# Attention and a squared-ReLU FFN in one planned order: batch 0's last P.V part, x turned pair by pair, and new constants of the planner

## The chip, the cores and the metric

The kernel runs on one core of a Trainium2 chip. The metric is the device time of one execution in microseconds (us), as the median of several runs. The core has a matrix engine (TensorE; PE in the profile, with its weight loads as PEld), VectorE (DVE), ScalarE (ACT), GpSimd (POOL) and SyncE (SP). Matrix products land in PSUM, of which the kernel uses eight banks of 128 x 512 fp32; DVE and ACT take them from there to SBUF. DMAs are issued here from POOL (nearly all loads, which turn fp32 into fp16 on the way), from SP (outputs, transposing DMAs, a few first loads) and from ACT (a few first loads).

## The reference, cut to what matters

Attention with a bias that depends on the distance of query and key, over 8 batches, 8 heads, 576 positions and head size 64; its heads laid side by side are the input of a two-layer FFN whose activation is the square of a ReLU.

```python
scores = scale * np.matmul(q, k.transpose(0, 1, 3, 2))      # q, k, v: 8 x 8 x 576 x 64
scores = scores + bias.transpose(2, 0, 1)[None, :, :, :]    # bias_table[bucket(|i - j|)]
attn = np.exp(scores - max); attn = attn / attn.sum(-1)
x = np.matmul(attn, v).transpose(0, 2, 1, 3).reshape(4608, 512)
h = np.maximum(x @ w_in, 0.0)                               # w_in: 512 x 2048
out = h * h @ w_out                                         # w_out: 2048 x 512
```

## The kernel before, in words

**The attention** goes by pairs of heads: pair p = 4 b + hp holds heads 2 hp and 2 hp + 1 of batch b, 32 pairs in all (`pair`, line 580). For each pair:

- q and k are loaded into a staging buffer (five of them, taken in order) and turned, so that the head size lies on the partitions. In batches 0 to 2 PE turns them with transposes (line 608): 12 of 96 x 64 for each of q and k, into a bank of the ring `r_g`, from which ACT or DVE copies them to SBUF (`copy_to`, lines 570 and 572). From batch 3 on, a transposing DMA of SP does it. POOL or DVE copies some 64 x 64 corners into `qz` (line 635). Pair 0's q and k come by their own loads as fp32 and are cast (lines 468 and 470).
- The scores are made by PE in the two banks-of-two `st` (lines 653, 677, 702) and taken through exp by ACT (lines 664, 687, 712) into `pt` and `pm`: four exps of 128 x 1024, one of 512 and one of 576 per pair.
- DVE multiplies them with exp(bias), only where keys and queries are near (four products per pair, line 745). The tables for it are built once at the start: far bias (326), 96 small matmuls (353) in six banks of `r_g`, copied to `tb_sb` by ACT or DVE (365, 367), and `tm_sb` (374).
- P.V is made by PE in two parts, query tiles 0 to 2 and 3 to 4 (lines 781 and 788), one after the other in the only bank `pv`, the row sums coming along as a 65th column. After each part DVE takes the reciprocal (805) and the product with it (810) into `x`.

**x** is then turned for the layers. In batches 0 to 2 (`x_turn`, line 838) this is done once per batch, after its fourth pair: for each of the five query tiles, four transposes, one per pair, into one bank of `r_g` (848), and one copy of up to 512 columns to `xt`. From batch 3 on SP's transposing DMA does it.

**The layers** go by nine groups of 512 tokens (`layers`, line 1026). Layer 1 of a group is 16 tiles; a tile is four matmuls over `kk`, that is over the four pairs of a batch, into one bank of `r_g` (1044), then ReLU by ACT or, in the first two groups, DVE (1065, 1067), then the square by DVE (1075). Layer 2 (`second`, line 929) uses a scheme with seven instead of eight products of 2 x 2 blocks, each product 16 matmuls (962). Sums of the activations (921) and of the weights (901) are made by DVE beforehand. Products 1 and 2, 5 and 3, and 7 and 4 follow one another in one bank each; 2, 3 and 4 have to wait until the one before has been read (989, 995, 997). Their order is `P_ORDER`, and `P_LAST` for the last group. Layer 2 of group g - 1 is interleaved with layer 1 of group g.

The ring `r_g` has three banks, and serves q and k turns, tables, x turns, layer 1 and layer 2 alike.

**The order of everything** is made before the program is built. Each piece of work is an `Op` with a cost per engine, what it depends on, the buffers that it takes, a due time and possibly an `after`, before which it may not be planned. `Plan.schedule` (line 106) advances each engine by itself and takes the op that can start first, and among several the one with the least due time. Ops that name two engines go to the one that can start first. The result is one fixed order on each engine. A pair's due time is `nominal(p)` = LEAD + FAST min(p, FASTN) + PERIOD max(p - FASTN, 0), its `after` is AHEAD earlier; group g is due at G0 + GP g. These constants set the priorities, and the costs in the `P.add` calls set the planner's clock; neither is a wait on the chip. The fills (memsets of constant regions, line 388, by DVE) have due times and `after` values of their own (QUIET, LATER, and 25000 for those of the staging buffers, line 405). The loads of POOL follow a list: those of batch 0, then `ORDER`, in which k0 and k1 are k of pairs 4, 5 and of pairs 6, 7 (q0 and q1 likewise), i0 to i3 quarters of w_in, o0 to o3 of w_out, and v the six loads of v of batch 1.

Of the kernel before, what the change touches and what calls it, by code (L numbers as in the profile page):

```python
# [25 lines left out]
GT = 512  # L26
# [4 lines left out]
PERIOD, LEAD, FAST, FASTN = 9600.0, 1600.0, 3000, 7  # L31
AHEAD, G0, GP = 20600.0, 54700.0, 35900.0
# [3 lines left out]
QUIET, LATER = 5200.0, 8500.0  # L36
TAB, EV = 6400.0, 1
P_ORDER = "1 6 2 5 7 3 4"
P_LAST = "1 6 2 5 7 3 4"
SIX = 3  # L40
ORDER = "k0 i0 q0 q1 v i1 i2 o0 k1 o1 i3 o2 o3"
# [149 lines left out]
def kernel(  # L191
# [74 lines left out]
    def loader(eng_name, eng, out_, in_, packets, deps=(), bufs=(), due=0.0):  # L266

        lane = [Buf(r_lane)] if eng_name == "POOL" else []
        issue = P.add(
            {eng_name: 720.0 if eng_name == "POOL" else 600.0},  # L270
            lambda: io(eng.dma_start(out=out_(), in_=in_())),  # L271
            deps,
            list(bufs) + lane,
            due,
        )
        return P.add({"DMA": packets / 16}, None, [issue], list(bufs) + lane, due if lane else -1e9), issue
# [9 lines left out]
    def load(eng_name, eng, out_, in_, packets, deps=(), bufs=(), due=0.0):  # L286
        return loader(eng_name, eng, out_, in_, packets, deps, bufs, due)[0]
# [15 lines left out]
        128 * 27, due=0,  # L303
# [21 lines left out]
        {"PE": 250.0},  # L325
# [21 lines left out]
    for c in range(6):  # L347
# [11 lines left out]
        o = P.add({"PE": 16 * 55.0}, t_mm, [o_eb, l_oh], [t_b], LEAD + TAB, 0.0, "f")  # L359
# [27 lines left out]
    def fill(ap, value, ns, due, after, deps=()):  # L387
# [3 lines left out]
    z_fix = [[fill(zz[:, 0], 0.0, 150.0, 10, QUIET)], [fill(zz[:, 1:], 0.0, 300.0, 11, LATER)]]  # L391
    first = [
        fill(pt_sb[:, :, PW:], 1.0, 150.0, 20, LATER),
        fill(pm_sb[:, :, S:], 1.0, 150.0, 20, LATER),
# [11 lines left out]
        fill(stg[i][w][96:128, 512:640].bitcast(FP32), 0.0, 90.0, 40 + i, 25000.0)  # L406
# [56 lines left out]
    def cast_first(w):  # L463

        def cast(o):
            src, dst = first_f[0:96, ts(w, 768)], stg[b_stg[0].slot][w][0:96, :]
# [95 lines left out]
    xt_ready, x_last = {}, {}  # L562
# [17 lines left out]
    def pair(p):  # L580
# [5 lines left out]
        for w, dst in ((0, qts), (1, kts)):  # L586
# [14 lines left out]
            def tr(w=w, bank=bank):  # L601
                ps = g_ps[bank.slot].bitcast(FP16)
                t = stg[b_stg[p].slot][w]
                if b < SIX:
# [11 lines left out]

            o = P.add({"PE": 12 * 36.0 if b < SIX else 5 * mm(128)}, tr, l_qk[p, w] + [l_id], [bank, b_stg[p]], T - 3000, after, "c" if b < SIX else "f")

# [152 lines left out]
        for part, qt0, nq in ((0, 0, 3), (1, 3, 2)):  # L771
            bank = Buf(r_pv)

            def pv(qt0=qt0, nq=nq, bank=bank):
                ps = pv_ps[bank.slot][:, 0 : nq * 130].rearrange("p (t e d) -> p t e d", t=nq, e=2)
# [27 lines left out]
            def recip(nq=nq, bank=bank, rb=rb):  # L803
                ps = pv_ps[bank.slot][:, 0 : nq * 130].rearrange("p (t e d) -> p t e d", t=nq, e=2)
                io(nc.vector.reciprocal(out=rs[rb.slot][:, 0:nq], in_=ps[:, :, :, 64:65]))

            def norm(nq=nq, bank=bank, rb=rb, qt0=qt0):
                ps = pv_ps[bank.slot][:, 0 : nq * 130].rearrange("p (t e d) -> p t e d", t=nq, e=2)
# [29 lines left out]
    def x_turn(b, norms):  # L838
        xb = [x_bufs[4 * b + hp] for hp in range(4)]
        T = nominal(4 * b + 3)  # L840
        for qt in range(5):
            n = 128 if qt < 4 else 64
            bank = Buf(r_g)

            def tr(qt=qt, bank=bank):
                ps = g_ps[bank.slot].bitcast(FP16)
                for kk in range(4):
                    io(nc.tensor.transpose(ps[:, ts(kk, 128)], xs[xb[kk].slot][:, qt, :], id_sb))  # L848

            deps = [n_[0 if qt < 3 else 1] for n_ in norms]  # L850
            o = P.add({"PE": 4 * mm(128)}, tr, deps, [bank] + xb, T, 0.0, "f")
            t0 = (b % XB) * S + qt * 128
            for a, z in [(0, n)]:
                c = t0 + a
                e = copy_to(
                    4 * (z - a),
                    lambda a=a, z=z, c=c: xt_sb[:, :, c : c + z - a],
# [281 lines left out]
```

The softmax here doesn't subtract the row's maximum and nothing guards it: scores larger than these inputs give would overflow.

## Time and profile before

| | us |
|---|---|
| median of 7 runs (lowest to highest) | 377.03 (376.30 to 377.43) |
| the profiled execution | 377.03 |
| its span, first to last instruction | 375.3 |
| busy in it: PE, PEld | 361.0, 246.7 |
| DVE, ACT, POOL | 268.9, 255.3, 180.3 |
| PE's first work (pair 0's turns, L608) | from 5.99 |
| first P.V | from 21.6 |
| first layer 1 tile | from 40.17 |
| last pair's last P.V matmuls | about 312 |
| last product of layer 2, start of its last matmul | 371.64 |

A busy time is the union of the spans of an engine's instructions. Matmuls are pipelined: one whose span is 0.38 us lets the next start after less than that, so PE's 96% is not yet a measure of how densely it works; for that the start times have to be read.

### The profile page before, as it was taken

The page shows a single profiled execution, that of the slowest core. Times are in us where ns is not written, and L with a number is a line of the kernel's source. Part 1 is how long each engine was busy: PE and PEld are TensorE (multiplying, and loading weights), DVE is VectorE, ACT ScalarE, POOL GpSimd, SP SyncE. Part 2 cuts the span into 40 slices and gives each one's busy share as a digit, 9 for nine tenths or more (in the row PEclk, how much of TensorE's full clock was granted, in tenths as well). Part 3 has the DMA queues.
Part 4 walks back from the last instruction along what each step waited for, and adds up shares of the span by engine and source line. Part 5 has one row for each costly group of instructions (what it writes and reads, how often), then busy time and mean ns, then how long its engine had stood idle before and what let it go on. Part 6 is the DMA issues. An engine that isn't in the chain of part 4 may idle for free.

```text
span 375.3 us, 10050 instructions
## 1 busy us (share of the span) xinstructions
PE 361.0 (96%) x4046; PEld 246.7 (66%) x4046; DVE 268.9 (72%) x612; ACT 255.3 (68%) x361; POOL 180.3 (48%) x318
## 2 busy tenths in 40 slices
PE   3988999999999999999999999999999999999996
PEld 2655456745778566687766665667577888556675
DVE  3896789998698586866685777757776683583653
ACT  4898889987656886866787778746885541464330
POOL 8877362889465592933858456754650000000000
PEclk9999999999999999999999999999999999999999
DMA  9999998799999799959999699999990222100103
GB/s 170 155 126 169 195 169 73 47 92 89 104 153 132 99 118 136 110 57 126 130 130 72 111 126 158 75 103 118 160 98 30 77 58 74 64 2 28 58 28 112
DMA packets 146163, 38.74 MB, mean 103 GB/s; under 512 B 128070, under 2 KB 146118, under 8 KB 146118
## 3 DMA queue, kind: packets, MB, share of 16 engines
q0 software_dynamic: 94496, 18.07, 60.8%
q1 hardware_dynamic: 51280, 19.75, 25.9%
q8 instruction: 31, 0.51, 0.6%
q10 hardware_dynamic: 342, 0.30, 0.3%
q14 instruction: 14, 0.11, 0.1%
HBM read 36.88 MB, written 9.44 MB: 123 GB/s over the span
## 4 chain that ended last, share of the span: by engine, by line
PE 90%; ACT 4%; DVE 2%; issue 1%; DMA 1%; ACTq 0%
PE f L1044 34%; PE f L962 29%; PE pv L788 9%; PE st L653 9%; PE pv L781 3%; PE st L702 2%; PE st L677 2%; PE f L608 1%; ACT pt L664 1%; DMA g<-in_k_dram 1%; ACT pt L687 1%; PE f L848 1%; ACT kt L570 0%; PE f L353 0%; DVE s L921 0%
## 5 line engine op out<-in xcount | busy, mean ns | idle before, releaser
L1044 PE MATMUL f<-xt,w_in_sb 128*128 128x512 f16 (+4 forms) x704 | 142.1, 341 | 0.0
L664 ACT ACTIVATE pt<-st 128x1024 f16<-128x1024 f32 x128 | 126.8, 1023 | 22.4 <-PE st L653 22.3
L1065 ACT ACTIVATE rt<-f 128x512 f16<-128x512 f32 x134 | 80.0, 598 | 62.0 <-PE f L1044 60.5
L1044 PEld LDWEIGHTS <-w_in_sb 128*128 128x128 f16 x704 | 62.5, 98 | 53.1 <-issue 10.8
L1075 DVE TENSOR_TENSOR g<-rt 128x512 f16<-128x512 f16 x144 | 60.8, 424 | 41.2 <-ACT rt L1065 40.1
L745 DVE TENSOR_TENSOR pt<-pt,tb_sb 128x1536 f16<-128x1536 f16 (+2 forms) x96 | 58.2, 621 | 10.6 <-ACT pt L664 9.9
L962 PEld LDWEIGHTS <-g 128*128 128x128 f16 x576 | 54.9, 98 | 15.4 <-issue 4.7
L788 PE MATMUL pv<-va,pt 128*128 128x65 f16 x1280 | 54.6, 193 | 0.0
L788 PEld LDWEIGHTS <-pt 128*128 128x128 f16 x1280 | 50.2, 97 | 2.9 <-issue 0.7
L271 POOL DMA_DIRECT2D qs<-in_q_dram x71 | 49.9, 724 | 1.9 <-POOLq L1123 0.9
L271 POOL DMA_DIRECT2D ks<-in_k_dram x71 | 50.1, 716 | 1.2 <-issue 1.2
L962 PEld LDWEIGHTS <-s 128*128 128x128 f16 x432 | 40.6, 98 | 10.6 <-issue 3.4
L635 POOL COPY qz<-qt 64x64 f16<-64x64 f16 x53 | 17.1, 323 | 59.5 <-DMA qt<-qs 31.8
L989 DVE SCALAR_TENSOR_TENSOR y<-f,y 128x512 f32<-128x512 f32 (+1 forms) x47 | 31.4, 667 | 16.1 <-PE f L962 15.1
L653 PE MATMUL st<-qt,kt 64*128 64x512 f16 x256 | 41.3, 392 | 1.3 <-ACT pt L664 0.5
L635 POOL COPY qz<-kt 64x64 f16<-64x64 f16 x59 | 20.7, 350 | 36.2 <-DMA kt<-ks 22.3
L962 PE MATMUL f<-wt,g 128*128 128x256 f16 x288 | 36.6, 273 | 0.0
L962 PE MATMUL f<-w_out_sb,s 128*128 128x256 f16 x288 | 36.6, 273 | 0.0
L962 PE MATMUL f<-w_out_sb,g 128*128 128x256 f16 x288 | 36.2, 273 | 0.1
L781 PE MATMUL pv<-vm,pm 128*128 128x130 f16 x160 | 35.3, 221 | 0.6 <-DVE x L810 0.4
L810 DVE TENSOR_TENSOR x<-pv,r 128x384 f16<-128x384 f32 x64 | 31.4, 490 | 1.9
L271 POOL DMA_DIRECT2D va<-in_v_dram x36 | 30.8, 862 | 0.0
(62 smaller groups left out, 307.2 us busy)
## 6 DMA issues: line engine op xcount, KB each, us to landing
out_dram<-y SPq DMA_DIRECT2D x34, 256.0 KB, 2.4
va<-in_v_dram POOLq DMA_DIRECT2D x28, 128.0 KB, 4.6
qs<-in_q_dram POOLq DMA_DIRECT2D x40, 64.0 KB, 3.1
ks<-in_k_dram POOLq DMA_DIRECT2D x40, 64.0 KB, 3.1
w_in_sb<-in_moe_w_in_dram POOLq DMA_DIRECT2D x4, 512.0 KB, 7.4
w_out_sb<-in_moe_w_out_dram POOLq DMA_DIRECT2D x4, 512.0 KB, 9.7
qs<-in_q_dram POOLq DMA_DIRECT2D x11, 144.0 KB, 5.5
ks<-in_k_dram POOLq DMA_DIRECT2D x11, 144.0 KB, 5.9
```

Source lines behind the costliest of these rows:

```text
L271: lambda: io(eng.dma_start(out=out_(), in_=in_())),
L635: io(eng.tensor_copy(out=dst[qb.slot][rw, rw], in_=src[qb.slot][rw, 512:576]))
L653: nc.tensor.matmul(sets_ps[st.slot][:, e, :], kt[rw, ts(jt, 128)], qt[rw, 0:512], start=True, stop=True,)
L664: nc.scalar.activation(out=p5(pts[pb.slot])[:, jt, :, 0:512], in_=sets_ps[st.slot], func=EXPF, scale=SCALE)
L745: io(nc.vector.tensor_tensor(out=a, in0=a, in1=t, op=MULT))
L781: nc.tensor.matmul(ps[:, i, :, :], pm[:, c : c + 128], vm[:, hp, :, 0:65], start=True, stop=False)
L788: nc.tensor.matmul(ps[:, i, e, :], pt[:, (2 * jt + e) * S + c : (2 * jt + e) * S + c + 128], va[:, jt, 2 * hp + e, 0:65], start=False, sto ...
L810: nc.vector.tensor_tensor(out=xs[xb.slot][:, qt0 : qt0 + nq, :].rearrange("p t (e d) -> p t e d", e=2), in0=ps[:, :, :, 0:64], in1=rs[rb.s ...
L962: nc.tensor.matmul(g_ps[bf.slot][:, ts(s_, HALF)], left(c, s_), right(c), start=(c == 0 and (s_ == 0 or apart) and i not in before), stop= ...
L1044: nc.tensor.matmul(g_ps[bank.slot][:, a:z], w_in_sb[:, kk, ts(nt, 128)], xt_sb[:, kk, c : c + z - a], start=(kk == 0), stop=(kk == 3),)
L1065: io(nc.scalar.activation(out=rts[rb.slot], in_=g_ps[bank.slot], func=RELUF))
L1075: nc.vector.tensor_tensor(out=gs[gb1.slot][:, nt, :], in0=rts[rb.slot], in1=rts[rb.slot], op=MULT)
```

## The change

- A second part of P.V in batch 0 takes a bank of `r_g` in place of the bank `pv`.
- x is turned after each pair, in two parts (three and two query tiles): three or two transposes into one bank, one copy of 384 or 192 columns. This is for batches 0 to 2.
- The first two tiles of layer 1 of group 0 are split: the matmuls of `kk` 0 to 2, which depend on the first three pairs, and that of `kk` 3 with the rest.
- Pair 0's cast puts q and k in another order, and its turns are six transposes of 96 x 128 in place of twelve of 96 x 64.
- q and k of pairs 1 to 4 are copied from PSUM by DVE alone (EV from 1 to 5; the copy is `dve_only` for 0 < p < EV).
- All fills may be planned from 0.9 us on (staging buffers from 0).
- Constants: due times of pairs, groups and tables, the order of loads, the order of the seven products, and planned costs (tables' matmuls, turns, far bias, fills, one load).

```diff
-PERIOD, LEAD, FAST, FASTN = 9600.0, 1600.0, 3000, 7
-AHEAD, G0, GP = 20600.0, 54700.0, 35900.0
+PERIOD, LEAD, FAST, FASTN = 9000.0, 0, 3000, 8
+AHEAD, G0, GP = 25000, 60000, 46000
-QUIET, LATER = 5200.0, 8500.0
-TAB, EV = 6400.0, 1
-P_ORDER = "1 6 2 5 7 3 4"
+QUIET, LATER = 900.0, 900.0
+TAB, EV = 5800.0, 5
+P_ORDER = "1 6 2 5 3 7 4"
 P_LAST = "1 6 2 5 7 3 4"
-ORDER = "k0 i0 q0 q1 v i1 i2 o0 k1 o1 i3 o2 o3"
+PV_G, PRE, FILL = 1, 2, 0
+ORDER = "k0 i0 q0 v i1 i2 q1 k1 i3 o0 o1 o2 o3"
...
-        {"PE": 250.0},
+        {"PE": 500.0},
         lambda: io(nc.tensor.matmul(g_ps[far_b.slot][:, 0:8], one_sb, far_sb, start=True, stop=True)),
...
-        o = P.add({"PE": 16 * 55.0}, t_mm, [o_eb, l_oh], [t_b], LEAD + TAB, 0.0, "f")
+        o = P.add({"PE": 16 * 33.0}, t_mm, [o_eb, l_oh], [t_b], LEAD + TAB, 0.0, "f")
...
-        fill(stg[i][w][96:128, 512:640].bitcast(FP32), 0.0, 90.0, 40 + i, 25000.0)
+        fill(stg[i][w][96:128, 512:640].bitcast(FP32), 0.0, 90.0, 40 + i, FILL)
...
-            src, dst = first_f[0:96, ts(w, 768)], stg[b_stg[0].slot][w][0:96, :]
+            src = first_f[0:96, ts(w, 768)].rearrange("p (e j d) -> p e j d", e=2, j=6)
+            dst = stg[b_stg[0].slot][w][0:96, :].rearrange("p (j e d) -> p e j d", e=2, j=6)
...
-                if b < SIX:
+                if p == 0:
+                    for j in range(6):
+                        io(nc.tensor.transpose(ps[:, ts(j, 96)], t[0:96, ts(j, 128)], id_sb[0:96, 0:96]))
+                elif b < SIX:
...
-            bank = Buf(r_pv)
+            bank, home = (Buf(r_g), g_ps) if b == 0 and part and PV_G else (Buf(r_pv), pv_ps)
...
-    def x_turn(b, norms):
-        xb = [x_bufs[4 * b + hp] for hp in range(4)]
-        T = nominal(4 * b + 3)
-        for qt in range(5):
-            n = 128 if qt < 4 else 64
-            bank = Buf(r_g)
-            def tr(qt=qt, bank=bank):
-                ps = g_ps[bank.slot].bitcast(FP16)
-                for kk in range(4):
-                    io(nc.tensor.transpose(ps[:, ts(kk, 128)], xs[xb[kk].slot][:, qt, :], id_sb))
-            deps = [n_[0 if qt < 3 else 1] for n_ in norms]
-            o = P.add({"PE": 4 * mm(128)}, tr, deps, [bank] + xb, T, 0.0, "f")
+    def x_turn(p, norms):
+        b, hp = divmod(p, 4)
+        xb = x_bufs[p]
+        T = nominal(p)
+        for part, qt0, nq in ((0, 0, 3), (1, 3, 2)):
             bank = Buf(r_g)
+            n = min(128 * nq, S - 128 * qt0)
+            c = (b % XB) * S + 128 * qt0
+            def tr(qt0=qt0, nq=nq, bank=bank):
+                ps = g_ps[bank.slot].bitcast(FP16)
+                for i in range(nq):
+                    io(nc.tensor.transpose(ps[:, ts(i, 128)], xs[xb.slot][:, qt0 + i, :], id_sb))
+            o = P.add({"PE": nq * mm(128)}, tr, [norms[part]], [bank, xb], T, 0.0, "f")
+            e = copy_to(
+                n,
+                lambda c=c, n=n: xt_sb[:, hp, c : c + n],
+                lambda bank=bank, n=n: g_ps[bank.slot].bitcast(FP16)[:, 0:n],
+                [o] + xt_free(b * S + 128 * qt0 + n), [bank], T,
+            )
+            for g_ in range((b * S + qt0 * 128) // GT, (b * S + qt0 * 128 + n - 1) // GT + 1):
+                xt_ready.setdefault(g_, []).append(e)
+                xt_pair.setdefault((g_, hp), []).append(e)
...
+                ahead = 3 if g == 0 and i < PRE else 0
+                o = None
+                if ahead:
+                    o = P.add(
+                        {"PE": ahead * mm(512)}, lambda f1=f1: f1(k1=3),
+                        [x for kk in range(ahead) for x in xt_pair[g, kk]] + [l_win[nt // 4]], [bank, gb1],
+                        due + i * 2000, 0.0, "f",
+                    )
                 o = P.add(
-                    {"PE": 4 * mm(512)}, f1, xt_ready[g] + [l_win[nt // 4]], [bank, gb1], due + i * 2000, 0.0, "f"
+                    {"PE": (4 - ahead) * mm(512)}, lambda f1=f1, ahead=ahead: f1(k0=ahead),
+                    [o] + xt_ready[g] + [l_win[nt // 4]], [bank, gb1], due + i * 2000, 0.0, "f"
                 )
```

## The prediction

> **What bounds the kernel.** I read the page's busy times and slices first, then the table by stages, the list of what PE waited for, and the timeline of the first 45 us.
>
> ```profile
> PE 361.0 (96%) x4046; PEld 246.7 (66%) x4046; DVE 268.9 (72%) x612; ACT 255.3 (68%) x361; POOL 180.3 (48%) x318
> PE   3988999999999999999999999999999999999996
> ```
>
> PE is full from the fifth slice to the last but one, so time can be won where it isn't dense, at both ends. A table of five stages (time, then busy us and instructions of PE, PEld, DVE, ACT, POOL, then clock, DMA share, GB/s) says how much is there:
>
> ```profile
> 6.00:16.70 10.70, 10.56 (x168) 6.97 (x168) 9.15 (x31) 7.99 (x11) 9.38 (x18) 1.00 1.54 174
> 16.70:40.17 23.47, 19.52 (x376) 13.91 (x375) 19.24 (x57) 21.87 (x32) 18.19 (x34) 1.00 1.27 148
> 40.17:361.70 321.53, 320.67 (x3415) 216.90 (x3413) 234.71 (x515) 222.74 (x317) 147.87 (x257) 1.00 0.86 98
> ```
>
> From 16.7 to 40.17 ACT is the fullest engine (21.87 of 23.47), DVE comes next, and PE is idle for 3.95; from 40.17 to 361.7 PE is idle for 0.86. Busy spans overlap, so I also priced every matmul by its usual distance from start to start in dense stretches: 0.216 us for a layer 1 matmul of 512 columns, 0.1095 for one of layer 2, 0.029 and 0.057 for those of P.V, 0.112, 0.1225 and 0.056 for the three kinds of scores, 0.0415 for a q or k transpose, 0.056 for one of x, 0.026 for a table's. All 4,046 come to 343.0 us. Of the span of 375.3, 32.3 are therefore not dense work: 5.9 before 6 us, 3.3 from 6 to 16, 7.0 from 16 to 40, 12.0 from 40 to 360 (0.04 per us), 4.1 after it. The change can touch the 10.3 us between 6 and 40 most; the first 5.9 are the first loads and casts.
>
> The head of PE's list of waits, and what happens before the first layer 1 tile (start, us, engine, line; "idle before" in brackets):
>
> ```profile
> PE f L608 <- DVE ks L470: 6.0, 1, 6.0
> PE st L702 <- ACT pt L664: 0.8, 1, 0.8
> PE f L848 <- DVE x L810: 0.6, 1, 0.6
> ```
>
> ```profile
> 23.59 1.21 ACT L570 ACTIVATE kt<-f 128x576 f16<-128x576 f16 x2
> ...
> 27.04 0.67 ACT L570 ACTIVATE qt<-f 128x576 f16<-128x576 f16 x1
> ```
>
> ```profile
> 33.18 0.59 ACT L687 ACTIVATE pt<-st 128x512 f16<-128x512 f32 x1
> ...
> 37.95 0.60 ACT L570 ACTIVATE xt<-f 128x512 f16<-128x512 f16 x1 [0.34 <-PE f L848]
> ```
>
> ```profile
> 34.78 0.22 PE L781 MATMUL pv<-vm,pm 128*128 128x130 f16 x1
> ...
> 37.07 0.84 PE L848 MATMUL f<-id_sb,x 128*128 128x128 f16 x12
> 37.75 0.22 PE L781 MATMUL pv<-vm,pm 128*128 128x130 f16 x1
> ...
> 39.25 0.45 PE L848 MATMUL f<-id_sb,x 128*128 128x128 f16 x5 [0.57 <-DVE x L810]
> 39.63 0.60 PE L653 MATMUL st<-qt,kt 64*128 64x512 f16 x4
> 40.17 2.76 PE L1044 MATMUL f<-xt,w_in_sb 128*128 128x512 f16 x12
> ```
>
> Layer 1 begins when batch 0 is through. Pair 3's last exp ends at 33.77. Its P.V's first part starts at 34.78, the second only at 37.75, since the one bank is held until the product with the reciprocal ends at 36.67 and other work stands ahead; then come reciprocal, product, transposes, copy: 6.4 us from the last exp to the first tile. Ahead of that, ACT's exps of four pairs run nearly without a gap from 15.8 on, with copies of q and k between them.
>
> **The change, part by part**, against the profiled execution (377.03; span 375.3 and 1.7 around it), which is also the median of the runs.
>
> *ACT's chain to pair 3's last exp.* Pairs 1 to 4 lose their ACT copies. Four stood in ACT's stream: at 8.34 (0.65), 11.98 (0.64), one of the two at 23.59 (0.60) and 27.04 (0.67). The last two count in full, 1.27: ACT is idle for nothing there. The first saves some 0.15, as the scores start only at 8.23; the second nothing, as the exp behind it waits for PE anyway. The table's copy at 17.78 (0.59) stands in the stream too; due 5800 in place of 8000 puts the tables ahead of pair 2, where DVE may take it: 0 to 0.6, I take 0.5. Pair 5's copies (0.60, 0.71) may stay on ACT: 0 to 1.3, I take 0.6. Sum 2.5, between 1.4 and 3.2: pair 3's exps end at about 31.3.
>
> *What DVE pays.* Four copies of 0.755 (rows of 128x576) are 3.0 us more. The fills leave DVE's busy stretch: 2.4 between 5.9 and 10.7, and ten at 25.13 that take 0.8 together, 3.2 in all; they go into DVE's idle 4.4 us before its first cast at 5.38. So DVE comes out level. x by pairs costs DVE 8 copies of (0.35 + 0.26)/2 by the line through its rows for 512 (0.42) and 256 columns (0.29), 2.4 in place of 2.0 per batch; that is spread over the pairs, and leaves the end of the chain. If DVE's cover is not there, the exps are early and the products with the tables late: a rival below.
>
> *From the last exp to layer 1.* Before 6.4. After: band product 0.48 and 0.1; P.V's two parts back to back 0.9 + 0.6 (the second in its own bank); reciprocal 0.18, product 0.42 and 0.25 of latencies; two transposes 0.3, a copy 0.29 and 0.1. Sum 3.6, and 0.5 for queueing on DVE: 4.1. Tiles 1 and 2 have their first six matmuls (1.3 us) ahead of that, as cover for PE. They hold two of three layers' banks, while pair 3's second P.V part and its two turns pass one after the other through the third, for about 1.5, 0.8 and 0.7 us. That is no longer than the chain itself; were it bare, it would cost up to 1.5. So the first tile is complete from 31.3 + 4.1 = 35.4 on, against 40.17.
>
> *What PE wins.* Not 4.8, since PE also worked in the meantime. The 2.5 us ahead of the exps' end are wall time with the same work in it, so they count. Behind it, 2.0 us were lost between 34 and 40; with 1.3 us of early tiles and a chain shorter by 2.3, I take 0.8 lost: 1.2 won. Sum **3.7**, between 1.4 (the first term's lower end alone) and 5.4 (3.2 + 2.2).
>
> *Pair 0's turn.* Six for twelve: at 5.99 twelve take 0.69 with two halves side by side. Nothing shown separates six full ones from it: -0.2 to +0.2, I take 0. The casts write the same 768 columns (0.84, 0.56) in runs of 64: 0, at most +0.2.
>
> *Loads.* q of pairs 6 and 7 (two issues of 0.64) go behind six loads of v, i1 and i2: 6.3 us later on POOL, and those 1.3 earlier. Pair 6's scores are at 50.7, so 0. i1 was issued at 28.02 and lands 7.4 later, at 35.4, now about 34.1; tile 4 needs it at about 39. i3 passes o0 and o1 (1.5 earlier, about 42 on landing; tile 12 came 16 us after tile 0, so about 51). w_out's first quarters come up to 2.8 later; their first reader is DVE at 73.4. All 0.
>
> *Due times.* Scores run far behind their `after`: pair 20's is 126.8, its scores are at 181.5. So AHEAD binds nothing in the middle; the two priorities, attention and layers, keep their order. 0, with bounds of 1.5 to both sides, an eighth of the 12.0 lost there.
>
> *Order of the products.* "5 3" and "7 4" now follow directly, and 3 and 4 must wait until DVE has read 5 and 7. Where no other work stands between, that is 0.16 us of matmul latency, 0.69 of reading (L989) and some 0.1 of signals: 1.0. There are 8 groups x 2 = 16 such places, 0 to 16 us. Before, another product of 1.75 us stood there. PE is dense in the middle because layer 1 tiles (0.87) and attention lie between; only from 305 to 314.6, while layer 1 of group 7 waits for pair 31, is layer 2 mostly alone. I take **0.6**, nearest to the dense middle.
>
> *At the attention's end.* If pair 31 comes no earlier, PE needs other work until 314.6. There were 40 matmuls of layer 2 left then, 4.4 us: enough for 3.7.
>
> Sum: 377.0 - 3.7 + 0.6 = **373.9**.
>
> **A rule against it.** Four score matmuls take 1.04 us at 12.15 and 0.60 at 24.31, and twelve transposes 0.69 at 13.12 and 0.45 at 17.50: PE's clock is low until about 17, although the stage table gives 1.00. The Trainium skill ("TensorE: Matmul & The Clock Gate", Part 1) says that full clock follows one busy window of about 3.4 us; by that rule the early stretch, with six transposes fewer per operand, could miss its window. An estimate from that page is half a window, 1.7 us, later or sooner. By the rows I leave the rise where it is.
>
> **Rivals.**
> - *Slower: bare product pairs.* Place: 5 to 3 and 7 to 4 in groups 0 to 7. For: PE cannot pass a waiting matmul, all behind it wait too, and DVE, which reads, is 73% busy in the middle. Against: tiles and attention lie between nearly everywhere. It decides from 4.5 of 16 places (3.7 + 0.75); with 6 bare: 377.0 - 3.7 + 6 = 379.3. Chance 0.14.
> - *No change.* DVE takes over as the bound of the front, and its added copies delay just what ACT's saved ones hasten: 376.3 to 377.8. Chance 0.10.
> - *Small gain.* DVE half binds, first tile at about 38; only the 1.4 remains: 377.0 - 1.4 + 0.2 = 375.8. DVE is 82% busy from 16.7 on, so this is near. Chance 0.17.
> - *Large gain.* Upper ends, 5.4 and an earlier clock or denser middle of 1: 370.6. For: 18 to 22 lost 2.3 us waiting for exps and tables, of which I counted little. Chance 0.17.
>
> Forecast, 372.5 to 375.3: 0.42. A measurement tells about 0.2% (0.75 us) from no change. Faster is 0.42 + 0.17 + 0.17 = 0.76, the same 0.10, slower 0.14. The range from 370.5 to 378.2 leaves out the slower rival's far part (about 0.12) and the large gain's end (0.05).
>
> **What will show it.** Right: pair 3's last exp ends near 31.3, the second P.V part starts within 1 us of the first, L1044 begins by 34 and is complete at about 35.4; no fills after 5.4; PE idle from 16.7 to the first tile under 3. Wrong: DVE without gaps and ACT waiting for it before 31; waits of L962 for DVE y (L989) in the middle; waits of L1044 for xt near 310; a score group of 1.04 us after 17.

## The result, and the profile after

The changed kernel takes 379.54 us (median of 20 runs, 379.05 to 381.23) against 377.30 in the runs made beside it: a ratio of 1.0063, with a 95% interval from 1.0054 to 1.0073. It is slower by 0.6%, where 373.9 us was predicted. The profiled execution spans 377.7 us, 2.4 more than before.

The page still shows PE as the fullest engine, with slightly more busy time for work of the same dense price:

```profile
PE 361.3 (96%) x4034; PEld 247.1 (65%) x4034; DVE 270.7 (72%) x616; ACT 254.2 (67%) x364; POOL 177.9 (47%) x320
PE   3989999799999999999999999999999999999996
```

The new thing is the 7 in the eighth slice, from 66 to 76 us. The three stages of the prediction (same columns) put the time in the third:

```profile
6.00:16.70 10.70, 10.18 (x160) 6.97 (x160) 7.00 (x17) 6.70 (x10) 9.19 (x18) 1.00 1.40 124
16.70:40.17 23.47, 20.51 (x358) 14.07 (x356) 19.49 (x52) 20.59 (x30) 18.67 (x33) 1.00 1.33 165
40.17:361.70 321.53, 318.40 (x3415) 215.59 (x3414) 233.75 (x514) 223.10 (x323) 145.18 (x260) 1.00 0.84 97
```

PE's idle time in the second stage fell from 3.95 to 2.96 us; in the third it rose from 0.86 to 3.13. The third stage cut finer, first before, then after (time, then busy us of PE, PEld, DVE, ACT, POOL):

```profile
60.00:65.00 5.00, 4.92 (x91) 2.92 (x89) 4.90 (x10) 4.92 (x9) 0.53 (x2) 1.00 0.41 24
65.00:70.00 5.00, 4.97 (x92) 3.88 (x92) 4.87 (x15) 4.97 (x8) 4.86 (x11) 1.00 0.99 65
70.00:75.00 5.00, 4.84 (x86) 3.67 (x83) 4.87 (x14) 5.00 (x10) 3.61 (x10) 1.00 0.36 24
```

```profile
60.00:65.00 5.00, 4.23 (x54) 2.61 (x54) 4.80 (x10) 4.78 (x7) 0.00 (x0) 1.00 0.05 3
65.00:70.00 5.00, 3.70 (x83) 2.96 (x83) 4.81 (x11) 2.74 (x5) 3.50 (x6) 1.00 0.62 42
70.00:75.00 5.00, 4.60 (x98) 3.49 (x97) 4.79 (x14) 4.35 (x8) 4.64 (x11) 1.00 0.49 30
```

DVE is full (96 to 98%) in both. Before, PE and ACT are nearly full too; after, PE runs short of work between 60 and 75 us (idle for 2.47 of the 15, before 0.27), and from 65 on ACT with it. This is the end of batch 1's attention: layer 1 of group 0 is through (its last tile starts at 60.4 before, 59.1 after), and group 1 has to wait for batch 1's x; it starts at 74.5 before and at 76.3 after.

To follow this through many kernels I use one measure, **loss**: the length of a stretch less the dense price of the matmuls in it, with the prediction's prices. All 343.04 us of work are the same before and after, so the loss is the whole difference. The losses of a kernel are those of its one profiled execution, the ratio is that of all its executions to the runs of before made beside them.

| kernel | lost to 45 us | 45 to 80 | 80 to 315 | ratio [95%] |
|---|---|---|---|---|
| before | 16.37 | 1.61 | 10.10 | 1 |
| after | 15.64 | 4.31 | 10.56 | 1.0063 [1.0054, 1.0073] |
| a_fills | 16.45 | 3.27 | 11.00 | 1.0080 [1.0055, 1.0104] |
| a_qkfirst | 15.86 | 4.09 | 12.73 | 1.0115 [1.0090, 1.0139] |
| a_times | 14.92 | 4.38 | 11.42 | 1.0077 [1.0051, 1.0104] |
| a_xbatch | 17.38 | 2.56 | 11.86 | 1.0069 [1.0043, 1.0096] |
| a_ev | 14.19 | 4.44 | 14.49 | 1.0092 [1.0069, 1.0115] |
| a_runf1 | 15.57 | 3.73 | 11.21 | 1.0068 [1.0044, 1.0093] |
| b_struct | 13.98 | 5.52 | 10.88 | 1.0099 [1.0064, 1.0135] |
| b_pvg | 15.94 | 4.43 | 10.57 | 1.0087 [1.0057, 1.0116] |
| a_pvg | 15.09 | 2.89 | 11.00 | 1.0045 [1.0029, 1.0061] |
| a_pvg_porder | 14.77 | 2.78 | 11.00 | 1.0021 [1.0001, 1.0040] |
| b_porder | 16.59 | 1.62 | 11.18 | 1.0022 [1.0002, 1.0042] |
| b_nudge3 | 17.45 | 3.69 | 10.44 | 1.0051 [1.0035, 1.0067] |
| b_nudge4 | 16.37 | 3.56 | 11.65 | 1.0070 [1.0051, 1.0089] |
| a_lessboth | 14.64 | 3.13 | 10.57 | 1.0003 [0.9989, 1.0017] |
| b_lessboth | 16.59 | 1.40 | 10.31 | 0.9986 [0.9971, 1.0000] |
| b_late6 | 16.37 | 3.85 | 10.49 | 1.0058 [1.0038, 1.0079] |
| a_q6 | 15.64 | 3.01 | 10.12 | 1.0019 [1.0004, 1.0034] |

Names that begin with a_ are the changed kernel with an edit, those with b_ the kernel before with one. After against before: 0.73 won to 45 us, 2.70 lost from 45 to 80, 0.46 behind that. By the same count the changed kernel is still 1.1 ahead at 60 us, so the loss falls between 60 and 80. a_quarter, below, does less work and is left out of the table.

### The profile page after: what moved, and what is told of

It is laid out like the page before. It is cut to its first block, busy times and chain, and to the rows that moved or that the text cites. A ratio compares the mean times of both kernels' runs of the same rounds, so it can differ in the third digit from the quotient of the medians.

```text
span 377.7 us, 10037 instructions
## 1 busy us (share of the span) xinstructions
PE 361.3 (96%) x4034; PEld 247.1 (65%) x4034; DVE 270.7 (72%) x616; ACT 254.2 (67%) x364; POOL 177.9 (47%) x320
## 4 chain that ended last, share of the span: by engine, by line
PE 89%; DVE 4%; ACT 4%; issue 1%; DMA 1%; ACTq 0%; DVEq 0%
PE f L1050 34%; PE f L968 29%; PE pv L796 9%; PE st L661 8%; PE pv L789 2%; ACT pt L672 2%; PE st L685 2%; PE st L710 2%; PE f L613 1%; DMA g<-in_k_dram 1%; DVE pt L753 1%; DVE qt L574 1%; PE f L354 1%; DVE x L818 1%; ACT rt L1080 0%
## 5 line engine op out<-in xcount | busy, mean ns | idle before, releaser
L672 ACT ACTIVATE pt<-st 128x1024 f16<-128x1024 f32 x128 | 126.3, 1024 | 22.5 <-PE st L661 22.5
L968 PEld LDWEIGHTS <-g 128*128 128x128 f16 x576 | 54.7, 98 | 15.3 <-issue 4.2
L796 PE MATMUL pv<-va,pt 128*128 128x65 f16 x1216 | 51.9, 193 | 0.0
L643 POOL COPY qz<-qt 64x64 f16<-64x64 f16 x60 | 19.0, 317 | 63.0 <-DMA qt<-qs 29.8
L968 PEld LDWEIGHTS <-s 128*128 128x128 f16 x432 | 40.5, 98 | 12.0 <-issue 4.7
L995 DVE SCALAR_TENSOR_TENSOR y<-f,y 128x512 f32<-128x512 f32 (+1 forms) x47 | 31.4, 668 | 17.1 <-PE f L968 16.1
L661 PE MATMUL st<-qt,kt 64*128 64x512 f16 x256 | 41.2, 390 | 2.1 <-ACT pt L672 1.7
L968 PE MATMUL f<-wt,g 128*128 128x256 f16 x288 | 36.7, 273 | 0.0
L968 PE MATMUL f<-w_out_sb,s 128*128 128x256 f16 x288 | 36.4, 273 | 0.0
L968 PE MATMUL f<-w_out_sb,g 128*128 128x256 f16 x288 | 36.4, 273 | 0.0
L789 PE MATMUL pv<-vm,pm 128*128 128x130 f16 x152 | 33.6, 221 | 1.2 <-DVE x L818 1.1
L643 POOL COPY qz<-kt 64x64 f16<-64x64 f16 x54 | 16.1, 299 | 35.2 <-DMA kt<-ks 31.8
L818 DVE TENSOR_TENSOR x<-pv,r 128x384 f16<-128x384 f32 (+1 forms) x60 | 29.7, 495 | 1.9
```

Source lines behind the costliest of these rows:

```text
L643: io(eng.tensor_copy(out=dst[qb.slot][rw, rw], in_=src[qb.slot][rw, 512:576]))
L661: nc.tensor.matmul(sets_ps[st.slot][:, e, :], kt[rw, ts(jt, 128)], qt[rw, 0:512], start=True, stop=True,)
L672: nc.scalar.activation(out=p5(pts[pb.slot])[:, jt, :, 0:512], in_=sets_ps[st.slot], func=EXPF, scale=SCALE)
L789: nc.tensor.matmul(ps[:, i, :, :], pm[:, c : c + 128], vm[:, hp, :, 0:65], start=True, stop=False)
L796: nc.tensor.matmul(ps[:, i, e, :], pt[:, (2 * jt + e) * S + c : (2 * jt + e) * S + c + 128], va[:, jt, 2 * hp + e, 0:65], start=False, sto ...
L818: nc.vector.tensor_tensor(out=xs[xb.slot][:, qt0 : qt0 + nq, :].rearrange("p t (e d) -> p t e d", e=2), in0=ps[:, :, :, 0:64], in1=rs[rb.s ...
```

## The experiments

### Single parts taken back from the changed kernel, and one order of loads

**a_fills**: the fills' old `after` values. **a_qkfirst**: q and k of pairs 1 to 3 ahead of v on POOL (not a part of the change: the kernel before has v between them too). **a_times**: old due times. **a_xbatch**: x turned once per batch, no early tiles. **a_ev**: copies of q and k open to ACT again.

```diff
a_fills
-QUIET, LATER = 900.0, 900.0
+QUIET, LATER = 5200.0, 8500.0
-PV_G, PRE, FILL = 1, 2, 0
+PV_G, PRE, FILL = 1, 2, 25000.0
a_times
-PERIOD, LEAD, FAST, FASTN = 9000.0, 0, 3000, 8
-AHEAD, G0, GP = 25000, 60000, 46000
-TAB, EV = 5800.0, 5
+PERIOD, LEAD, FAST, FASTN = 9600.0, 1600.0, 3000, 7
+AHEAD, G0, GP = 20600.0, 54700.0, 35900.0
+TAB, EV = 6400.0, 5
a_ev
-TAB, EV = 5800.0, 5
+TAB, EV = 5800.0, 1
a_qkfirst
-        if hp == 2:
-            load_v_tail(0)
-        if hp >= 1:
-            for h in range(2 * hp - 2, 2 * hp):
-                load_v_head(0, h)
-    for h in range(6, 8):
+    load_v_tail(0)
+    for h in range(8):
         load_v_head(0, h)
a_xbatch (and x_turn of the kernel before)
-PV_G, PRE, FILL = 1, 2, 0
+PV_G, PRE, FILL = 1, 0, 0
-        for p in range(4 * b, 4 * b + 4):
-            norms = pair(p)
-            if b < DT_X:
-                x_turn(p, norms)
+        norms = [pair(4 * b + hp) for hp in range(4)]
+        if b < DT_X:
+            x_turn(b, norms)
```

> The changed kernel with the old earliest times of all fills (5.2, 8.5 and 25 us). It leaves out nothing of the computation. Theory L (loads): the early fills let POOL issue v of batch 0 before q and k of pairs 2 and 3 (those went from 3.9-5.4 to 4.2-11.8 us), and this kept ACT waiting; then pair 3's last exp comes before 33 us in place of 34.45, and the time falls by 1 to 2 us from 379.5. Theory G (gate): the time is set by when x of batch 1 is in place (layer 1 of group 1 from 76.3, before 74.5), and only a move of that counts: time minus 379.5 = that start minus 76.3, within 0.7 us. Rival C (constants): no effect of the fills, 379.5 within 0.7.

> The changed kernel with the first loads in another order on POOL: q and k of pairs 1 to 3 first, then all of v of batch 0. Theory L: ACT's stalls between 7 and 22 us shrink, pair 3's last exp comes about 2 us sooner than 34.45, and the time falls by 1 to 2 us. Theory G: what counts is the start of layer 1 of group 1 (76.3): if that stays within 0.5, so does the time, whatever the first batch does. Rival C: 379.5 within 0.7.

> The changed kernel with the old due times of pairs, groups and tables. Rival C (constants): the due times are what made it slower, so the time falls to 377.3 or below, by 2 us and more. Theory G: the time follows the start of layer 1 of group 1; which way that moves with the old due times it doesn't say, but time minus 379.5 = that start minus 76.3, within 0.7 us. Theory L: no change, 379.5 within 0.7, as the early loads stay as they are.

> The changed kernel with x turned once per batch again, as before, and without the split tiles that need it by pairs. Rival X: 24 copies and turns in place of 15, on the fullest engines and the three shared banks, are what made it slower; then the time falls by 1.5 to 2.5 us. Theory G: the start of layer 1 of group 0 goes from 39.0 to about 41 and this costs nothing; the time follows the start of layer 1 of group 1 within 0.7 us. The prediction's own view: layer 1 of group 0 later by 2 costs about 1 us, so 380.5.

> The changed kernel with the copies of q and k of pairs 1 to 4 free to go to ACT or DVE again. Theory G, form D (DVE is what binds up to batch 1's x): DVE loses some 3 us of copies ahead of 76, layer 1 of group 1 starts by 75, and the time falls by 1 to 2 us. Theory G, form B (banks): within 0.7 of 379.5. Rival P: ACT's chain in batch 0 gets longer by 1.3 to 2.5 us, and the time rises by about as much.

Measured: 380.75, 381.95, 380.41, 380.43 and 380.76 us. None is faster than the changed kernel. The front did move: the loss to 45 us lies between 14.2 and 17.4. But at 80 us it is between 18.6 and 20.0 in all of them. So what the front wins is given back behind it, and none of these five edits by itself brings the time back. The constant `ORDER`, the list of loads, was not taken back alone.

Two of the theories fail here. Theory L wanted pair 3's last exp before 33 us; it ends at 35.52 in a_fills and 34.91 in a_qkfirst, later than the changed kernel's 34.45. Theory G wanted the time to follow the start of group 1's layer 1 within 0.7 us; in a_ev that start is 75.0, 1.3 earlier than after, and the time is 1.2 longer, and in a_qkfirst 0.3 of delay goes with 2.4. That start alone is therefore no measure of the time. What is left of theory G is that DVE and ACT lead up to batch 1's x.

### The structure without the constants

**b_struct** is the kernel before with the second P.V bank, x by pairs, early tiles and pair 0's turn, and all constants, loads and costs as before.

```diff
+PV_G, PRE, FILL = 1, 2, 25000.0
... (pv, recip, norm, x_turn, cast_first and layers as in the changed kernel; no other constant)
```

> The kernel before with the four edits of structure alone (pair 0's turn in six, the second bank for P.V of batch 0, x by pairs, the two early tiles), and all constants, costs, fills and orders as before. If structure is what costs (theory G, form B): 379 to 380.5, and the dense work done by 80 us is 60 to 60.7. If the constants are (rival C): 377.3 or less, as the front's gain of about 1 us remains.

Measured: 380.94. It has the earliest front of all (13.98 lost to 45 us, with the granted clock at full from 11.3 us in that execution, against 16.7 before) and the largest loss behind it, 5.52. So the loss is there without the new constants.

### The second P.V bank and the products' order, each by itself

```diff
a_pvg
-PV_G, PRE, FILL = 1, 2, 0
+PV_G, PRE, FILL = 0, 2, 0
b_porder
-P_ORDER = "1 6 2 5 7 3 4"
+P_ORDER = "1 6 2 5 3 7 4"
b_pvg (and home in place of pv_ps in pv, recip and norm)
-            bank = Buf(r_pv)
+            bank, home = (Buf(r_g), g_ps) if b == 0 and part else (Buf(r_pv), pv_ps)
```

a_pvg_porder is a_pvg with `P_ORDER = "1 6 2 5 7 3 4"` besides.

> The changed kernel with the second part of batch 0's P.V back in its own single bank; the rest of the change stays. So far all four variants of the changed kernel had done the same dense work by 80 us (60.1 to 60.7 us of it; the kernel before 62.0), whatever the first tile's time. Theory G (gate: batch 1's x, bound by ACT and DVE together): the three layers' banks are the scarce thing between 20 and 76 us, a bank held by P.V through reciprocal and product delays q and k turns of batch 1; without it layer 1 of group 1 starts by 75 and the time falls to about 378. Rival P (the prediction's view): the second bank hastens the front, so without it the first complete tile comes 1 us later and the time rises to 380 to 381.

> The kernel before with one edit of the change alone: the second part of batch 0's P.V in a layers' bank. Rival P (the prediction's step): the second part no longer waits for the first's product, the first layer 1 tile comes 1 to 2 us sooner than 40.2, and the time falls by about 1 us. Theory G: the first tile may come sooner, but PE's earlier work gets in the way of the scores that feed ACT; layer 1 of group 1 starts later than 74.5 by 1.5 to 2.5 us, and the time rises by 1 to 2 us.

> The kernel before with the products' order 1 6 2 5 3 7 4 in place of 1 6 2 5 7 3 4, nothing else. The prediction's slower rival (product pairs that stand bare): 1 us for every bare place, 379 or more, and waits of layer 2 on DVE's reading in the list of waits. Theory G: the first 90 us are the same as before, and the time is within 0.7 of 377.3.

> The changed kernel with two parts undone: the second P.V bank, and the order of the seven products. One by one, the first took 0.9 us off the change's 2.2, and the second put 0.8 on the kernel before. If the two are all of it: 377.3 to 377.9. If other parts cost too (x by pairs, loads, copies on DVE): 378.3 or more.

Measured: 378.67, 380.30, 378.41 and 378.20. The second bank alone makes the kernel before slower by 0.87%; without it the changed kernel is at 1.0045. Not all of the 0.87% is the bank's: five of the six executions of b_pvg have a mean granted clock of 0.991 or 0.995, which goes with a stretch at half clock (last section), against 7 of the 24 of before made beside them. The one without took 379.50, those of before without it 377.09, so by that one execution the bank's part is nearer to 0.6%. Rival P, a gain of 1 us, is refuted all the same. The products' order costs about 0.2%, some 0.8 us, both alone and taken back on top of a_pvg; with an interval from 0.02 to 0.42% that is at the limit of what can be told. It is more than theory G's 0.7 us and less than the 1.7 or more of the bare pairs. With both undone the rest of the change costs 0.2% (up to 0.4%), though its front is 1.6 us ahead at 45 us: 1.2 of these are gone by 80, the rest, and 0.5 more, by 315.

The bank is held for a reason of the front, but the loss lies between 45 and 80 us, in batch 1, where P.V does not use it. So not the bank, but something that follows from it, had to be looked for.

### Is PE the bound up to 75 us?

**a_quarter** makes layer 1 of group 0 with `kk` 3 alone, order kept: 48 matmuls of 0.216 us, 10.4 us of PE's work, are left out. (G in its expectation: this layer is only filler there.) **a_runf1** (S: the order of pair scores) plans the first run of scores of each pair of batch 1 ahead of that pair's last keys and queries.

```diff
a_quarter
-                        for kk in range(k0, k1 if z > a else 0):
+                        for kk in range(max(k0, 3) if g == 0 else k0, k1 if z > a else 0):
a_runf1 (ran holds the pair's runs; the same for spread[2:4])
-score, evac + spread[0:2], [st, qb, pb], T, after, "f")
+score, evac + spread[0:2] + (ran[:1] if b == 1 else []), [st, qb, pb], T, after, "f")
```

> The changed kernel in the same order, but layer 1 of group 0 does a quarter of its matmuls (kk 3 alone, 16 tiles of one matmul in place of four); what it leaves out is 48 matmuls of 512 columns, 10.4 us of PE at 0.216. If PE's dense work sets the time also before 76 us (the accounting of the prediction): the time falls by 9 to 10.4 us, to 369 to 370.5. Theory G: layer 1 of group 1 starts at most 2 us sooner than 76.3, because exps and DVE lead to it, and the time falls by at most 2.5 us, to 377 or more.

> The changed kernel; in batch 1 the first two score tiles of a pair are planned ahead of that pair's scores for the last queries and keys, nothing else. In the changed kernel pair 6's scores start at 56.1, behind four small groups of pairs 6 and 7 (before: 50.7, ahead of them). Theory G, form S (late scores of pair 6 are what delays batch 1's x): they start near 51, layer 1 of group 1 near 74.5 to 75.3, time 378 to 378.8. If the last exps of pair 7 come no sooner than at 68 all the same (DVE binds): 379.5 within 0.7.

Measured: 376.57 (0.998 [0.996, 1.000]) and 379.61. Of 10.4 us taken from PE only 3.0 come off the time, and group 1 starts at 73.5, 2.8 sooner; both are a little more than theory G allowed (2.5 and 2), and far from the 9 to 10.4 of the other view. In a_runf1 pair 6's scores start at 50.2 as wanted, but pair 7's last wide exp ends at 68.5, no sooner than after (68.3), and nothing is won: form S fails, and its "DVE binds" fits. What remains full in a_quarter is shown by its stages:

```profile
40.00:48.00 8.00, 6.66 (x114) 3.89 (x113) 7.87 (x20) 8.00 (x13) 1.74 (x6) 1.00 1.21 198
48.00:56.00 8.00, 6.10 (x75) 3.38 (x74) 7.86 (x22) 8.00 (x15) 5.85 (x10) 1.00 1.28 202
56.00:64.00 8.00, 6.29 (x98) 3.93 (x99) 7.86 (x17) 5.98 (x9) 0.94 (x3) 1.00 0.95 77
```

DVE is at 98%, ACT at 100% in two of the three; PE has 19.05 of 24. So part of PE's "96%" is, in this stretch, filler: DVE and ACT set the pace, with batch 1's exps and products and with the ReLUs and squares of layer 1, which a_quarter still does.

**a_lessboth** and **b_lessboth** leave part of the exps and products out instead, order kept:

```diff
-tt(view(0, [[S, 2], [1, 256]]), tab(128, 256, 1))
+tt(view(0, [[S, 2], [1, 32 if b == 1 else 256]]), tab(128, 32 if b == 1 else 256, 1))
... (384 and 320 columns likewise)
-[:, jt, :, 0:512], in_=sets_ps[st.slot],
+[:, jt, :, 0 : 256 if b == 1 else 512], in_=sets_ps[st.slot][:, :, 0 : 256 if b == 1 else 512],
```

> The changed kernel with its order kept; in batch 1 (pairs 4 to 7) the products with the table cover an eighth of their columns and the exps of 1,024 columns only 512 of them, which is left out of the computation: by the rows some 5.4 us less of VectorE and 6.8 us less of ScalarE between 36 and 76 us; TensorE's work is the same. Theory F (those two engines feed TensorE there): the 4.3 us that TensorE loses from 45 to 80 us shrink to 1.5 or less, layer 1 of group 1 starts 2 to 3 us earlier than 76.3, time 376.0 to 377.5. Rival T (order alone): no gain, 379 to 380.

> The same cut in the kernel before, order kept. Theory F: TensorE loses only 1.6 us from 45 to 80 us there, so 0.3 to 1.6 us are to be had: 375.5 to 377.0, clearly less than the changed kernel gains from the same cut. Rival T: nothing, 377.0 to 377.6.

Measured: 377.80 and 377.28. The changed kernel gains 0.6% from this. The kernel before gains 0.14%, which is nothing: without the executions that have a stretch at half clock, 377.14 stand against 377.22. F's direction holds for the changed kernel: with DVE and ACT relieved, most of what the change cost is gone. Its sizes were too large: both times lie above its ranges, and from 45 to 80 us the loss fell by 1.2 (4.31 to 3.13), not to 1.5, though group 1 starts 2.3 sooner (73.98). Another 1.0 of the 2.2 is in the stretch up to 45, and 0.7 of it is there by 36 us, where a_lessboth and the changed kernel still run the same instructions in the same order; the clock was granted in full from 14.3 us on in place of 16.1.

### Is it any new order at all?

**b_nudge3** and **b_nudge4** are the kernel before with one planned cost changed by a few per cent. The work is the same; the order differs, and with it a few pieces that may go to either of two engines have changed theirs (ACT has 365 and 362 instructions in place of 361).

```diff
b_nudge3
-            o = P.add({"DVE": 200.0}, recip, [o], [bank, rb], T - 2000)
+            o = P.add({"DVE": 220.0}, recip, [o], [bank, rb], T - 2000)
b_nudge4
-            o = P.add({"PE": 12 * 36.0 if b < SIX else 5 * mm(128)}, tr, ...
+            o = P.add({"PE": 12 * 37.0 if b < SIX else 5 * mm(128)}, tr, ...
```

> The kernel before with one price of the planner changed, the reciprocal's from 200 to 220 ns; every instruction is the same, only the order differs. Rival T: 378.5 to 381, so 0.4 to 1% lost by a new order as such. Theory F: within 0.3% of before, 376.5 to 378.3, because no engine's load has changed.

> The kernel before with another price of the planner changed, a q or k transpose's from 36 to 37 ns; every instruction is the same, only the order differs. Rival T: 378.5 to 381. Theory F: 376.5 to 378.3.

Measured: 379.53 and 380.28, as rival T said: an order that differs for no reason costs as much as the change. But not every new order does: a_pvg_porder is at 1.002, and so is b_porder, whose order is that of before up to 103 us. In the traces, both nudged kernels and b_pvg have in common with the changed kernel where pair 6's last queries (the four matmuls of L677 before, L685 after) stand: ahead of pair 6's second run of scores (L653 or L661), at 51 to 55 us, where before has them behind it at 57.4. In a_pvg, a_pvg_porder and b_porder they are behind, as before. This is a correlation, and a loose one: a_pvg, at 1.0045, cannot be told from b_nudge3 at 1.0051.

### The swap made, and undone

```diff
b_late6
-score, evac, sets + [qb, pb], T, after, "r")
+score, evac, sets + [qb, pb], T, 58500.0 if p == 6 and jts == [2, 3] else after, "r")
a_q6 (runs_of[6] holds pair 6's two runs, the first and the second)
+BEHIND_K = lambda p: runs_of[6][:1] if p == 6 else runs_of[6][1:] if p == 7 else []
+BEHIND_Q = lambda p: runs_of[6][1:] if p == 6 else runs_of[6][1:] if p == 7 else []
-score, evac + spread[0:2], [st, qb, pb], T, after, "f")
+score, evac + spread[0:2] + BEHIND_Q(p), [st, qb, pb], T, after, "f")
... (spread[2:4] with BEHIND_K likewise)
```

> The kernel before, with one due time changed: pair 6's second run of scores is held back by some 2 us in the planner's order, so that the last-query scores of pair 6 and the last-key scores of pair 7 come ahead of it; all up to 53 us is in the order of before. Theory K (this swap is what costs): second run at 57 to 59 us in place of 55.3, layer 1 of group 1 from 76 us on or later, time 378.8 to 381. If another stretch causes the loss: 377 to 378.2.

> The changed kernel, with the second P.V bank and all else kept, but pair 6's scores put in the order first run, last keys, second run, last queries, and pair 7's last keys and queries behind them, as in the kernel before. Theory K: pair 6's second run at 55 to 57 us in place of 60.3, layer 1 of group 1 at about 75, TensorE's loss up to 80 us 18.5 or less in place of 19.95, time 377.5 to 378.7. Rival T or another cause in that stretch: 379 to 380.5.

Measured: b_late6 379.63, a_q6 377.95. Both come as theory K said, but for a_q6's loss up to 80 us, 18.65 where 18.5 was named. The swap, with all that the planner then orders anew behind it, costs the kernel before 0.58%; undone in the changed kernel, it brings the ratio from 1.0063 to 1.0019. PE's timeline, before and then b_late6 (start, us, engine, line):

```profile
53.01 0.41 PE L702 MATMUL st<-qt,qz 128*128 128x288 f16 x2
...
55.08 0.60 PE L653 MATMUL st<-qt,kt 64*128 64x512 f16 x4
...
57.35 0.39 PE L677 MATMUL st<-qz,kt 128*128 128x128 f16 x4
...
59.04 0.41 PE L702 MATMUL st<-qt,qz 128*128 128x288 f16 x2
```

```profile
53.04 0.41 PE L702 MATMUL st<-qt,qz 128*128 128x288 f16 x2
...
55.02 0.39 PE L677 MATMUL st<-qz,kt 128*128 128x128 f16 x4
55.24 0.41 PE L702 MATMUL st<-qt,qz 128*128 128x288 f16 x2
...
57.31 0.61 PE L653 MATMUL st<-qt,kt 64*128 64x512 f16 x4
```

Up to 55 us the two agree within 0.1 us, on PE, DVE and ACT. Then pair 6's second run is 2.2 us later (in the changed kernel it starts at 60.07). What follows is seen on DVE, whose products with the reciprocal end each P.V part; before, then b_late6, then after, pair 7's two parts:

```profile
70.75 0.56 DVE L810 TENSOR_TENSOR x<-pv,r 128x384 f16<-128x384 f32 x1
...
72.59 0.42 DVE L810 TENSOR_TENSOR x<-pv,r 128x256 f16<-128x256 f32 x1
```

```profile
72.37 0.56 DVE L810 TENSOR_TENSOR x<-pv,r 128x384 f16<-128x384 f32 x1
...
74.75 0.42 DVE L810 TENSOR_TENSOR x<-pv,r 128x256 f16<-128x256 f32 x1
```

```profile
72.55 0.56 DVE L818 TENSOR_TENSOR x<-pv,r 128x384 f16<-128x384 f32 x1
...
74.41 0.42 DVE L818 TENSOR_TENSOR x<-pv,r 128x256 f16<-128x256 f32 x1
```

Batch 1's x is finished 2 us later, and on an engine that is 96 to 98% full this is not caught up; group 1's layer 1 starts at 78.1 in b_late6, 76.3 after, 75.3 in a_q6, 74.5 before. PE is short of other work by then: from 60 to 75 us it is idle for 1.48 in b_late6, 2.47 after and 0.27 before.

The swap is not all that differs, though. Behind 55 us the order of b_late6 departs from before's in many places, and seven instructions have gone from DVE to ACT. Its last wide exp of pair 7 even ends sooner (66.27, before 66.78). The delay is on DVE: from 45 us to the end of pair 7's last product it does 31.4 us of work, before 29.1, because work of others, above all pair 8's widest product, a copy of k, a ReLU and a sum of weights, now stands ahead. So it is shown that one due time, which puts pair 6's second run behind, makes the planner write an order that costs 2.3 us; which of the places of that order costs it is not separated.

**What stays open.** The swap is not the only way to a late batch 1. a_xbatch has the old order of pair 6, but a later front (17.38) and is slow. a_runf1 has pair 6's second run at 56.4, as early as a_q6, and wins nothing; its second run of pair 7 is at 66.1, 2.3 later than in a_q6. a_ev, at 18.63 lost to 80 us, loses 4.4 more than before behind it; its profiled execution is the slowest of its four, with a wait of 2.13 us and a stretch at half clock (last section). Which of the edits' effects in the planner's choice puts the last queries ahead was not traced. a_q6 still loses 1.4 more than before from 45 to 80, and with the old order of the products besides it was not run. No version that does all the work and beats the kernel before was found.

## Why the prediction was wrong

- **The miss in sum.** 373.9 was forecast and 379.5 measured, 5.6 us more. Of these 3.0 are missing in the front (0.7 won up to 45 us in place of 3.7) and 2.7 are lost from 45 to 80, which the sum did not have; the 0.5 behind that is about the 0.6 that it had for the products.
- **What failed** is the step "What PE wins", first in its size, by the term from ACT's chain (below), and then in the sentence "The 2.5 us ahead of the exps' end are wall time with the same work in it, so they count". It takes a gain of the front as a gain of the end, and no step looked at what lies between 45 and 80 us. There DVE and ACT have a fixed amount of work for batch 1, and PE beside it only layer 1 of group 0, 64 matmuls or 13.8 us: begun earlier, it ends earlier, and the wait for batch 1's x grows. a_quarter (3.0 of 10.4 us), b_struct (2.4 us ahead at 45, 1.5 behind at 80) and a_pvg_porder (1.6 ahead, 0.2% slower in time) bear it out.
- **What was missing** is the price of a new order there. The second P.V bank was costed at the front alone; it costs 0.2% by a_pvg and 0.6 to 0.9% by b_pvg. By a_q6, which keeps the bank and wins 0.4% with another order, most of this comes from the order that the planner then makes 15 us later.
- *ACT's chain*, 2.5 us won, also failed: pair 3's last exps end at 34.45, 0.7 later than before. The copies did leave ACT (busy from 8 to 68 us 50.5 in place of 54.0), but what they left is idle time before the 1024-wide exps, waiting for scores, 5.0 us in place of 0.8, of which 2.8 fall ahead of pair 3's last exp. Two of ACT's groups in that stretch, first before, then after (line, engine, tiles, shapes, count, then busy us and mean ns, then idle time before them and what ended it):

```profile
L664 ACT ACTIVATE pt<-st 128x1024 f16<-128x1024 f32 x32 | 31.7, 1028 | 0.8 <-PE st L653 0.8
...
L365 ACT ACTIVATE tb_sb<-f 128x512 f16<-128x512 f32 x1 | 0.6, 592 | 0.0
```

```profile
L672 ACT ACTIVATE pt<-st 128x1024 f16<-128x1024 f32 x32 | 31.6, 1032 | 5.0 <-PE st L661 5.0
...
L366 ACT ACTIVATE tb_sb<-f 128x512 f16<-128x512 f32 x3 | 1.7, 597 | 0.4 <-PE f L354 0.4
```

  And ACT has three table copies, 1.7 us, where it had one of 0.6 and was expected to have none. The scores of pairs 1, 2 and 3 begin 0.6, 2.0 and 2.0 us later than before. a_ev gives the copies back to ACT, and from 20 to 45 us it loses 5.1 us where the changed kernel loses 5.0: there the move of the copies, which the prediction put at 1.3 or more, was worth nothing that shows. Which of the edits makes the scores of pairs 1 to 3 late stays open.
- *From the last exp to layer 1*: right. 4.1 forecast, 4.6 measured (34.45 to 39.02, before 6.4); the second part follows the first at once, 35.96 after 35.07.
- *The front as a whole*: 3.7 forecast, 0.7 measured at 45 us, 1.1 at 50.
- *What DVE pays*: level or better (26.4 us busy from 6 to 40 us, before 28.4). *Due times* at 0: no gain from taking them back. *Loads* at 0: no run takes their order back alone; b_struct, which has the old one, is slow as well.
- *Order of the products*: 0.6 forecast, some 0.8 us measured alone (0.1 to 1.6). The rival of bare pairs did not come: after's list of PE's waits has no wait of L968 on DVE's y, and what was named as its price, 6 us, is not there. The slower side was given 0.14, for the wrong mechanism.
- *No change*: DVE as the next bound was named, but for the front, with its price set at what the front had won.
- *The clock*: six transposes fewer did not miss the window; it was granted in full from 16.1 us on, before from 16.7.

## What to carry to other kernels

A full engine is the bound only in those stages where it does work that the end waits for; ask stage by stage what its next work waits for, and carry a gain of one stage through the next one before counting it. Where a planner writes the order, an edit also costs what the new order costs elsewhere: run two or three meaningless changes of its prices first, because the loss that they bring (here 0.5 and 0.7%, the two that were tried) is what an edit's effect must be told from. And when kernels differ for no visible reason, compare the order of instructions at the place where the loss begins, then make that one swap in the good kernel, and see how much more the planner has changed with it.

## What the runs showed of the hardware

The granted clock can fall back in the middle of a kernel after short gaps. In b_pvg PE waited 0.52 and 0.53 us between 30.6 and 32.0, was busy for only 2.83 of the 4 us from 28 on, and from 32.9 ran at half clock for 3.41 us (the clock is the column behind POOL's):

```profile
28.00:32.00 4.00, 2.83 (x56) 1.99 (x53) 3.65 (x12) 4.00 (x7) 3.55 (x9) 1.00 0.91 123
32.00:36.00 4.00, 3.55 (x46) 3.04 (x46) 2.04 (x7) 2.26 (x4) 2.94 (x6) 0.61 1.22 192
36.00:40.00 4.00, 3.66 (x44) 2.44 (x42) 2.33 (x7) 3.11 (x5) 2.00 (x3) 0.96 1.23 193
```

In a_ev one wait of 2.13 us for a transposing DMA, which ended at 194.3 us, was followed by 3.41 us at half clock from 195.1 on, 0.68 from 196 to 200. b_nudge3 has such a stretch from 21.8 on, behind waits of 0.52 and 0.53 us that end at 19.2 and 20.1. The profiled execution of before has the same two waits at 19.9 and 20.8 and no fall, so the gaps alone do not decide it. The Trainium skill ("TensorE: Matmul & The Clock Gate", Part 1, What's actually happening) puts the fall behind an idle window of about 3.4 us; no gap here was that long, so these rows go further than that sentence. The profiled executions of b_pvg, a_ev and b_nudge3 have a mean granted clock of 0.995, all others 0.998 or more and no such stretch before their end. Of the 99 executions of the kernel before that were made beside the experiments, 31 have 0.994 or 0.995; their median is 378.28 us, that of the others 377.16. So executions with such a stretch are about 1.1 us longer, and a median moves with how many of them it has.

Full clock was first granted anywhere from 10.8 to 17.4 us after the span's start in the profiled executions. a_lessboth and the changed kernel, the same up to 36 us, had it from 14.3 and 16.1 on and differ by 0.7 us there, so a single profile's front is uncertain by about that much for this reason alone.
